# A first stage written as a table of steps, in a kernel of linear attention and a gated unit

## The chip, the core and the metric

One of the eight cores of a Trainium2 chip runs the kernel. The metric is the device time of one execution in microseconds (us), given as the median of several runs. PE is the matrix engine (TensorE), DVE the vector engine, ACT the scalar engine, POOL is GpSimd, and SP is the engine whose queue issues all DMA transfers of this kernel.

## The reference, cut to what matters

```python
xn = _layernorm(x, axis=-1)
qkv = (xn @ wqkv).reshape(B, S, 3, H, Dh)       # S 2048, D 1024, H 32, Dh 32
pq, pk = q @ w_phi, k @ w_phi                   # per head
phi = concat(softmax(p), softmax(-p))           # for q and k
num, den = phi_q (phi_k^T v), phi_q sum(phi_k)
s = (num / den).reshape(B, S, D) @ wo
g = silu((sigmoid(xn @ w_gate) * (xn @ w_up)) @ w_down)   # F 3584
return x + s * g
```

All of it is fp32. The tokens are taken in two chunks of 1024.

## The kernel before, in words

**Products.** Every large product is cut into 2 x 2 blocks, and seven block products, named B11, B21, T2, T3, T4, T1 and B22, take the place of eight; T1 to T4 and B22 have sums of blocks as operands. An fp32 operand is split in two: ACT casts it to its upper half (the helper `split`, L176), DVE subtracts that from the operand and so gets the lower half (L177). `mm3` (L181 to L183) then makes upper x upper, upper x lower and lower x upper. A block product of the first stage has four tiles of 128 tokens with four slices of depth 128 each, so 4 x 4 x 3 = 48 PE products of 128x512. Its results go to one PSUM bank for each tile (`banks[0]` to `banks[3]`) and are evacuated by `proj_out`, by ACT for B11 and B21 (L474, L477), by DVE for the others (L471).

**The first stage.** The first seven of the list `ops` are the block products of V for the first chunk; K's and Q's follow. Beside them the kernel makes ready what they need:

- It loads x in eight tiles of 128 x 1024 (`xk`). Each is normalized: `norm_steps` has DVE take the statistics (L211, L212), then a chain of small steps (L214 to L223) and a scaling of the tile, on ACT (L227) or DVE (L229). PE transposes it in two halves with four transposes each (L249). The halves of tiles 0 to 3 are split from PSUM as operands of B11 and B21 and copied to SBUF (L252). From tiles 4 to 7 and these copies, sums are made for T3 and T2 (`x_tiles`, on POOL), T4 and T1 (`x_late`, on POOL).
- It loads V's weights in four blocks of 1 MB (`v_load`) and makes four sums of them (`v_sums`, L302): three on DVE and T2's on POOL. Each sum is stored to `wf_d` (L303).
- It folds `w_phi` into the weights of K and Q. `fold(which, k)` loads four pieces of 256 KB (`fold_load`, L340), multiplies each by a block-diagonal `bd` on PE (four fp32 products of 128x128, L354, which the profile shows as 8 rows: a fold group), copies the four results to SBUF on ACT (L356, L358), makes two sums on DVE and two on POOL (L79) and stores seven blocks to `wf_d` (L345). There are four folds for K and four for Q.

**What sets the order.** The code puts x's first tile and its first product in front, with 44 transposes of an identity before them (`keep_going`, L844), and the rest into a queue `side`; `step()` runs one entry of it behind each tile of a block product. The helper `Pieces` cuts POOL's sums in pieces of 256 columns (L79). Weights are split ahead by `prep`, in a ring of eight slots. A scheduler then orders the instructions of each engine by its own estimates, but only where data, buffers or an explicit "issue after" leave it a choice. Each engine runs its own list in order; SP too, so that a transfer waits for all that stands before it in SP's list.

Of the kernel before, what the change touches and what calls it, by code (L numbers as in the profile page):

```python
# [17 lines left out]
P = 128  # L18
S, D, H, DH, F = 2048, 1024, 32, 32, 3584
KT = D // P  # L20
# [71 lines left out]
B11, T2, T3, B21, T1, T4, B22 = range(7)  # L92


@with_exitstack
def hedgehog_glu_kernel(
# [92 lines left out]
    side, last_sp = deque(), []  # L189
# [14 lines left out]
    def norm_steps(tiles, xs, scale=None):  # L204
# [20 lines left out]
        for i, xt in enumerate(xs):  # L225
            if scale is None:
                nc.scalar.activation(xt, xt, AF.Identity, bias=b[:, i:i + 1], scale=r[:, i:i + 1])  # L227
            else:
                scale(xt, xt, r[:, i:i + 1], b[:, i:i + 1], op0=ALU.mult, op1=ALU.add)  # L229

    def norm(tiles, xs, scale=None):
        for _ in norm_steps(tiles, xs, scale):
            pass

    def operand(c, i, u, b):

        if c == 0:
            o, cs = run(XO[i], 4), slice(u * P, (u + 1) * P)
            split((o[:, :, 0, cs], o[:, :, 1, cs]), b.rearrange("p (k t) -> p k t", t=P))
        else:  # L240
            nc.sync.dma_start(xo_d[i, :, u], b)

    def transpose(t, xt, dst):

        th, u = t // 4, t % 4
        for q in range(2):
            tp = tps.next()
            for k in range(4):
                nc.tensor.transpose(tp[:, k * P:(k + 1) * P], xt[:, (4 * q + k) * P:(4 * q + k + 1) * P], ident)  # L249
            if th == 0:  # L250
                operand(0, (B11, B21)[q], u, tp)
            nc.scalar.copy(dst[q], tp)  # L252
# [28 lines left out]
    fblock = {K: Ring(((4, 5), (6, 7))), Q: Ring(((50, 51), (52, 53)))}  # L281
# [9 lines left out]

    def v_load(i):
        r, f, kh = ((39, 0, 0), (41, 0, 1), (45, 1, 0), (36, 1, 1))[i]
        nc.sync.dma_start(row4(r), v_block(f, kh))

    def v_sums(*which):
        vec, pl = nc.vector.tensor_tensor, pool.tensor_tensor
        for t, f, o, a, b, op in ((T1, vec, 3, 2, 3, ALU.add), (T3, vec, 2, 0, 2, ALU.subtract),
                                  (T2, pl, 0, 3, 0, ALU.subtract), (B22, vec, 1, 1, 0, ALU.subtract)):
            if t in which:  # L300
                for h in range(2):
                    f(whole(VA[o] + h), whole(VA[a] + h), whole(VA[b] + h), op=op)  # L302
                nc.sync.dma_start(wf_d[V, t], row4(v_first[t]))  # L303
# [29 lines left out]

    fold_raw = {}

    def fold_load(which, k):
        for n in range(4):
            r = fraw.next()
            fold_raw.setdefault((which, k), []).append(r)
            last_sp[:] = [nc.sync.dma_start(r, wqkT[which, n // 2, k + 4 * (n % 2)].rearrange("p g n -> p (g n)")).ins]  # L340

    def fold(which, k):

        def keep(i, b):
            nc.sync.dma_start(wf_d[which, i, :, k], b)  # L345

        if (which, k) not in fold_raw:
            fold_load(which, k)
        a11, a12, a21, a22 = bs = halves(*fblock[which].next())
        for n, (b, r) in enumerate(zip(bs, fold_raw[which, k])):  # L350
            ps = tps.next()
            for g in range(4):
                gs = slice(g * P, (g + 1) * P)
                nc.tensor.matmul(ps[:, gs], r[:, gs], bd[:, 4 * (n // 2) + g], start=True, stop=True)  # L354
            if which == Q:
                nc.scalar.copy(b.rearrange("p (a g d) -> p g a d", a=2, d=DH), ps.rearrange("p (g a d) -> p g a d", a=2, d=DH))  # L356
            else:
                nc.scalar.copy(b, ps)  # L358
        for i, b in ((B11, a11), (B21, a12), (T4, a22)):
            keep(i, b)  # L360
        if k < 3:
            fold_load(which, k + 1)
        vector.add(a22, a21, a22)
        pool.sub(a21, a11, a21)
        vector.sub(a11, a22, a11)
        pool.sub(a12, a12, a11)
        with tc.issue_after(last_sp[0]):
            for i, b in ((T2, a11), (T1, a22), (T3, a21), (B22, a12)):
                keep(i, b)
# [461 lines left out]

    XS = (24, 25, 26, 27, 52, 53, 24, 25)
    first = [halves(i) for i in (50, 51, 54, 38)]
    b12s, b22s = Ring(halves(10)), halves(8, 9)
    xts = [x_load(0, XS[0])]
    v_load(0)
    xts += [x_load(t, XS[t]) for t in range(1, 4)]
    v_load(1)
    xts += [x_load(t, XS[t]) for t in range(4, 6)]

    def keep_going(n):

        for _ in range(n):
            nc.tensor.transpose(banks[3][:, :P], ident, ident)  # L844

    def x_norm(*tiles, scale=None):
        norm(tiles, [xts[t] for t in tiles], scale)

    def x_tiles(*tiles):
        for t in tiles:  # L850
            if t < 4:
                transpose(t, xts[t], first[t])
            else:
                u = t - 4
                (b11, _), (b12, b22) = first[u], (b12s.next(), b22s[u])
                transpose(t, xts[t], (b12, b22))
                pool.sub(b12, b22, b12)
                operand(0, T3, u, b12)
                pool.add(b11, b12, b11)
                operand(0, T2, u, b11)  # L860
            if t < 2:
                xts.append(x_load(t + 6, XS[t + 6]))
            if t == 1:
                v_load(2)
                v_load(3)

    def x_late():
        for u, (b11, b21) in enumerate(first):
            pool.sub(b21, b21, b11)
        block("x6", XO[T4], 4, F32R)  # L870
        for u, (b11, b21) in enumerate(first):
            operand(0, T4, u, b21)
        for u, (b11, b21) in enumerate(first):
            pool.sub(b11, b22s[u], b11)

    def x_rest():
        for i, name, src in ((B22, "x1", b22s), (T1, "x2", [b[0] for b in first])):
            block(name, XO[i], 4, F32R)
            for u in range(4):
                operand(0, i, u, src[u])  # L880
        fraw.items = halves(43, 54)

    with tc.high_priority():
        keep_going(44)
        x_norm(0, scale=nc.vector.tensor_scalar)
        x_tiles(0)
        x_norm(1)
    while prep():
        pass
    one = whole(44)[:, :P]  # L890
    nc.gpsimd.memset(one, 1.0)
    nc.scalar.copy(ones, one)
    phraw = whole(47)[:, :KT * DH].rearrange("p (g f) -> p g f", f=DH)
    nc.sync.dma_start(phraw, w_phi.rearrange("(g p) f -> p g f", p=P))
    nc.gpsimd.memset(bd, 0.0)
    for j in range(4):
        nc.gpsimd.tensor_copy(bd[j * DH:(j + 1) * DH, :, j * DH:(j + 1) * DH], phraw[j * DH:(j + 1) * DH])

    def todo(f, *a, **kw):
        side.append(lambda: f(*a, **kw))  # L900
# [387 lines left out]
```

## Time and profile before

| | |
|---|---|
| median of 3 runs | 2368.73 us (2367.17 to 2371.69) |
| the profiled execution's own time | 2370.45 us |
| its span, first to last instruction | 2368.7 us |
| PE busy | 2346.8 us (99%) |
| DVE, ACT, POOL busy | 1656.8, 992.8, 1189.1 us (70%, 42%, 50%) |
| mean granted clock of PE | 0.997 |
| moved by DMA | 626.24 MB, mean 264 GB/s |

In rows of groups, "out<-in" are the names of tiles, then come shapes, the count, busy time and mean time of one, and the idle time of the engine just before them with what ended it. In rows of stretches each engine has its busy time and, in parentheses, its instructions; then come the granted clock, the share of the 16 DMA engines and GB/s. A busy PE is not PE at its peak, since its products are pipelined: 390 ns are shown for a product, while the next one starts after about 227.

### The profile page before, as it was taken

What the parts mean: (1) busy time and instruction counts of PE and PEld (TensorE: products, weight loads), DVE (VectorE), ACT (ScalarE), POOL (GpSimd) and SP (SyncE); (2) the same over time, 40 slices, a digit from 0 to 9 for tenths busy, and PEclk for the clock granted to TensorE, in tenths of its full rate; (3) what the DMA queues carried; (4) which work ended last, traced back from release to release, by engine and by line L of the source; (5) the groups of instructions that cost most, each with busy time, mean ns of one, the idle gap of its engine ahead of it and who ended that gap; (6) DMA issues with size and microseconds to landing.
All of it is one profiled execution on the core that took longest, in us unless ns stands there. A gap on an engine that the chain in (4) does not pass through costs nothing. (4 is left out here: it accounts for less than half of the span.)

```text
span 2368.7 us, 32568 instructions
## 1 busy us (share of the span) xinstructions
PE 2346.8 (99%) x10772; PEld 1953.9 (82%) x10772; DVE 1656.8 (70%) x2360; ACT 992.8 (42%) x1478; POOL 1189.1 (50%) x1362
## 2 busy tenths in 40 slices
PE   8999999999999999999999999999999999999999
PEld 7788888878888788888888888888888888888887
DVE  7644788677777676466867878776666676667886
ACT  6432344444554454233434344443434333355442
POOL 4510166768776633304363544555444455633767
PEclk9999999999999999999999999999999999999999
DMA  8875566888887889858888877879777877878665
GB/s 299 271 260 175 163 236 220 277 294 300 306 307 275 299 288 364 311 178 275 271 282 274 293 268 259 284 253 356 249 241 260 269 237 244 288 255 291 227 210 168
DMA packets 266427, 626.24 MB, mean 264 GB/s; under 512 B 37905, under 2 KB 66577, under 8 KB 261649
## 3 DMA queue, kind: packets, MB, share of 16 engines
q1 hardware_dynamic: 266256, 624.15, 77.4%
q8 instruction: 85, 1.39, 0.2%
q14 instruction: 86, 0.70, 0.1%
HBM read 374.47 MB, written 249.56 MB: 263 GB/s over the span
## 5 line engine op out<-in xcount | busy, mean ns | idle before, releaser
L182 PE MATMUL bank<-x,w 128*128 128x512 f32 x2352 | 916.2, 390 | 0.0
L181 PE MATMUL bank<-x,w 128*128 128x512 f32 x2352 | 904.9, 390 | 4.5 <-DVE fb L1052 3.3
L183 PE MATMUL bank<-x,w 128*128 128x512 f32 x2352 | 905.8, 389 | 0.0
L79 POOL TENSOR_TENSOR fc<-fc 128x256 f32<-128x256 f32 x494 | 426.7, 894 | 443.1 <-DMA fc<-e_d 105.9
L176 ACT CAST w<-fa 128x512 fp32r<-128x512 f32 (+1 forms) x444 | 308.2, 698 | 561.7 <-PE bank L182 353.2
L177 DVE TENSOR_TENSOR w<-fa,w 128x512 fp32r<-128x512 f32 (+1 forms) x444 | 404.5, 913 | 197.2 <-ACT w L176 191.2
L181 PEld LDWEIGHTS bank<-x,w 128*128 128x128 f32 x2352 | 441.9, 188 | 98.0 <-DVE fb L1052 4.2
L183 PEld LDWEIGHTS bank<-x,w 128*128 128x128 f32 x2352 | 442.1, 188 | 91.6
L182 PEld LDWEIGHTS bank<-x,w 128*128 128x128 f32 x2352 | 442.2, 188 | 90.4
L181 PE MATMUL bank<-w,x 128*128 128x512 f32 x704 | 276.0, 392 | 2.4 <-ACT w L176 1.6
L183 PE MATMUL bank<-w,x 128*128 128x512 f32 x704 | 275.9, 392 | 0.9 <-DVE x L177 0.9
L182 PE MATMUL bank<-w,x 128*128 128x512 f32 x704 | 275.6, 391 | 1.0 <-DVE w L177 1.0
L79 POOL TENSOR_TENSOR fb<-fa 128x256 f32<-128x256 f32 x112 | 100.1, 914 | 244.3 <-DMA fa<-w_gu 143.7
L79 POOL TENSOR_TENSOR fb<-fb,fc 128x256 f32<-128x256 f32 x132 | 122.5, 949 | 115.9 <-DVE fc L1059 115.7
L181 PEld LDWEIGHTS bank<-w,x 128*128 128x128 f32 x704 | 132.7, 189 | 30.4 <-ACT w L176 2.1
L183 PEld LDWEIGHTS bank<-w,x 128*128 128x128 f32 x704 | 132.8, 189 | 28.9 <-DVE x L177 1.8
L182 PEld LDWEIGHTS bank<-w,x 128*128 128x128 f32 x704 | 132.7, 189 | 27.9 <-DVE w L177 1.5
L79 POOL TENSOR_TENSOR fc<-fc,sa 128x256 f32<-128x256 f32 x128 | 97.0, 789 | 98.6 <-issue 89.2
L176 ACT CAST p<-fc 128x512 fp32r<-128x512 f32 x100 | 75.6, 758 | 135.4 <-DVE fc L537 68.4
L177 DVE TENSOR_TENSOR p<-fc,p 128x512 fp32r<-128x512 f32 x100 | 102.0, 1024 | 32.0 <-ACT p L176 31.8
L177 DVE TENSOR_TENSOR x<-fa,x 128x512 fp32r<-128x512 f32 x112 | 92.0, 822 | 41.8 <-ACT x L176 41.8
L176 ACT CAST w<-fb 128x512 fp32r<-128x512 f32 (+1 forms) x114 | 71.2, 626 | 116.7 <-PE bank L182 91.4
(210 smaller groups left out, 2917.3 us busy)
## 6 DMA issues: line engine op xcount, KB each, us to landing
ws_d<-w SPq DMA_DIRECT2D x112, 512.0 KB, 4.3
w<-ws_d SPq DMA_DIRECT2D x112, 512.0 KB, 5.3
fa<-w_gu SPq DMA_DIRECT2D x84, 512.0 KB, 4.8
fa<-h_d SPq DMA_DIRECT2D x84, 512.0 KB, 4.9
fa<-wf_d SPq DMA_DIRECT2D x32, 1024.0 KB, 6.6
h_d<-fc SPq DMA_DIRECT2D x120, 256.0 KB, 4.7
fa<-w_down SPq DMA_DIRECT2D x80, 256.0 KB, 5.0
h_d<-fb SPq DMA_DIRECT2D x76, 256.0 KB, 4.7
```

What stands on the lines that cost most here:

```text
L79: last = self.engine.tensor_tensor(o[:, s], a[:, s], b[:, s], op=op)
L176: nc.scalar.copy(o[0], src)
L177: return nc.vector.tensor_sub(o[1], src, o[0].bitcast(F32))
L181: nc.tensor.matmul(o, a[0], b[0], start=first, stop=False, **kw)
L182: nc.tensor.matmul(o, a[0], b[1], start=False, stop=False, **kw)
L183: nc.tensor.matmul(o, a[1], b[0], start=False, stop=last, **kw)
```

## The change: a table in place of the code's order

A string `FIRST` now lists some 390 steps of the first stage in one order. A loop gives each to `now(what)`, within `turn()`: every instruction that a step makes must be issued behind the last instruction that earlier steps put on the same engine. So each engine keeps the table's order, SP included; instructions from outside the table may still be put between.

The table covers B11, B21, T2, T3 and T4 of V (products in half depth: "a" is upper x upper, "b" the other two), all of x, the folds 0 to 2 of K with their sums and stores (`f`, `fc`, `k`, `kp`, `ks`), the sums of V's weights and their stores (`v`, `vst`) and the splits of T1's weights and operands (`wcast T1`, `wsub T1`, `scast t1`, `ssub t1`). The loop over `ops` skips the first five. K's fold 3 and the four of Q stay in `side`. Further: x's second tile is loaded first and the first in two halves, V's first two blocks in halves; `w_phi` comes in a layout in which one transfer of 128x256 suffices; two of the four copies to `bd` go to ACT; tile 0, 1, 4 and 5 are scaled on DVE, the others on ACT; K's folds have four sets of buffers (two before); V's sum for T1 is made on POOL and T2's on DVE; of the 16 sums of x, DVE makes 14 and POOL 2.

```diff
+FIRST = """
+x1, bn 1 0, x0a, bn 1 1, x0b, bn 0 0, wphi, x3, diag 1, ag 1, add 1, bn 0 1, sqrt 1, diag 0, ag 0, r01, add 0, c 1
...
+    @contextmanager
+    def turn():
+        traced = nc.cur_bb.bb.instructions
+        mark = traced[-1]
+        with ExitStack() as behind:
+            for i in list(turns_last.values()):
+                behind.enter_context(tc.issue_after(i))
+            yield
+        start = next(k for k in reversed(range(len(traced))) if traced[k] is mark) + 1
+        for i in traced[start:]:
+            turns_last[i.engine] = i
...
-    fblock = {K: Ring(((4, 5), (6, 7))), Q: Ring(((50, 51), (52, 53)))}
+    fblock = {K: Ring(((4, 5), (6, 7), (52, 53), (50, 51))), Q: Ring(((52, 53), (50, 51)))}
...
+        elif kind == "v":
+            i, h, p = map(int, a[:3])
...
+            if a[3] == "P":
+                nc.gpsimd.tensor_tensor(columns(o, p), columns(l, p), columns(m, p), op=op)
+            elif p == 3:
+                nc.vector.tensor_tensor(o, l, m, op=op)
...
+        elif kind == "vst":
+            i = (T2, B22, T3, T1)[int(a[0])]
+            nc.sync.dma_start(wf_d[V, i], row4(v_first[i]))
...
+    for what in FIRST.replace("\n", " ").strip().split(", "):
+        with turn():
+            now(what)
+    flow.update(item=12, made=24, used=20)
+    fraw.items = halves(43, 54)
     while prep():
         pass
...
+    for w, k in [(K, 3)] + [(Q, k) for k in range(4)]:
+        side.append(lambda w=w, k=k: fold(w, k))
...
         if kind == "proj":
+            if n < 5:
+                continue
...
-        "w_phi": f(A_w_phi).reshape(D, DH),
+        "w_phi": f(np.asarray(A_w_phi).reshape(KT, P, DH).transpose(1, 0, 2)).reshape(P, KT * DH),
```

**Where instructions move.** In the names below `bank_98` to `bank_105` are the eight PSUM banks, `x_0_92` holds raw tiles of x, `x_0_90` and `x_0_91` are the operands of B11 and B21, `w_93` the split weights, `fa_95`, `fb_96`, `fc_97`, `p_94`, `x_0_87` and `x_0_88` buffers of the first stage. First PE at the start, before:

```order
L844 MATMUL bank_101<-ident 128x128 x44
L249 MATMUL bank_102<-ident,x_0_92 128x128 x4
L249 MATMUL bank_103<-ident,x_0_92 128x128 x4
L987 MATMUL bank_98<-w_93,x_0_90 128x512 x12
L181 MATMUL bank_98<-w_93,x_0_91 128x512
L182 MATMUL bank_98<-w_93,x_0_91 128x512
L183 MATMUL bank_98<-w_93,x_0_91 128x512
```

And PE at the start, now:

```order
L1038 MATMUL bank_101<-ident 128x128 x43
L329 MATMUL bank_105<-fb_96 128x128 x3
L1038 MATMUL bank_101<-ident 128x128
L329 MATMUL bank_105<-fb_96 128x128
L329 MATMUL bank_102<-fb_96 128x128 x4
L977 MATMUL bank_103<-ident,x_0_92 128x128 x4
L977 MATMUL bank_104<-ident,x_0_92 128x128 x4
L995 MATMUL bank_98<-w_93,x_0_90 128x512 x2
L329 MATMUL bank_105<-fb_96,x_0_88 128x128 x4
L977 MATMUL bank_102<-ident,x_0_92 128x128 x4
L995 MATMUL bank_98<-w_93,x_0_90 128x512 x4
```

Two fold groups of K stand before the first tile's transposes, and the first tile's products are cut in pieces with folds and transposes between; before, the first fold came behind product 96.

Second POOL, from the fills of `bd` on, before:

```order
L897 COPY fb_96<-fc_97 32x8x32 x4
L79 TENSOR_TENSOR fa_95<-p_94,fa_95 128x256 x8
L79 TENSOR_TENSOR x_0_88<-x_0_88 128x256 x2
L79 TENSOR_TENSOR fc_97<-x_0_88,fc_97 128x256
L79 TENSOR_TENSOR x_0_88<-x_0_88 128x256 x2
L79 TENSOR_TENSOR fc_97<-x_0_88,fc_97 128x256
L79 TENSOR_TENSOR fc_97<-fc_97 128x256
```

POOL at the same place, now:

```order
L942 COPY fb_96<-fc_97 32x8x32 x2
L1014 TENSOR_TENSOR p_94<-fb_96,p_94 128x256 x8
L79 TENSOR_TENSOR x_0_87<-x_0_87 128x256 x2
L1028 TENSOR_TENSOR fc_97<-fc_97 128x256 x2
L79 TENSOR_TENSOR x_0_87<-x_0_87 128x256 x2
L1028 TENSOR_TENSOR fc_97<-x_0_88,fc_97 128x256
```

The sums of x (`x_0_88`, `fc_97`) have left POOL but for two; counted up to Q's first fold POOL has 22 pieces of 128x256 where it had 56. DVE, behind the scaling of tile 4, now:

```order
L970 TENSOR_SCALAR fc_97<-fc_97,norm_108 128x1024
L1016 TENSOR_TENSOR fb_96<-fa_95,fb_96 128x1024
L970 TENSOR_SCALAR fc_97<-fc_97,norm_108 128x1024
L1030 TENSOR_TENSOR x_0_88<-x_0_88 128x512
L1030 TENSOR_TENSOR fc_97<-x_0_88,fc_97 128x512
L1030 TENSOR_TENSOR fc_97<-fc_97 128x512
```

There the sums of x stand, each in one piece of 512 columns (L1030).

Third SP at the start, before:

```order
L201 DMA x_0_92<-xk 128x1024
L294 DMA fa_95<-wv 128x4x512
L201 DMA x_0_92<-xk 128x1024 x3
L294 DMA fa_95<-wv 128x4x512
L201 DMA fc_97<-xk 128x1024 x2
L894 DMA fc_97<-w_phi 128x8x32
L294 DMA fb_96<-wv 128x4x512
L294 DMA p_94<-wv 128x4x512
```

SP at the start, now:

```order
L259 DMA x_0_92<-xk 128x1024
L928 DMA x_0_92<-xk 128x512 x2
L924 DMA fc_97<-w_phi 128x256
L259 DMA x_0_92<-xk 128x1024
L323 DMA fb_96<-wqkT 128x512 x2
L938 DMA fa_95<-wv 128x2x512
L323 DMA x_0_88<-wqkT 128x512
L938 DMA fa_95<-wv 128x2x512
```

The weights of K's first fold and the small `w_phi` now stand in front of V's second half block; V's first half block stands behind 2.2 MB of other transfers, where the whole block was second. From the 653rd PE instruction on (of 10646) PE's order is the same in both programs; this is behind product 415 and K's, and all of Q's, last fold.

More of the change, by code (lines that the diff above doesn't have):

```diff
@@ L225, in norm_steps @@
         for i, xt in enumerate(xs):
[L226 to L233, printed above, removed]
-    def operand(c, i, u, b):
[L237 to L252, printed above, removed]
+            nc.scalar.activation(xt, xt, AF.Identity, bias=b[:, i:i + 1], scale=r[:, i:i + 1])
+    def operand(c, i, u, b):
+        nc.sync.dma_start(xo_d[i, :, u], b)
     def x_sums(u, first, second):
@@ L867, in x_late @@
[L867 to L881, printed above, removed]
@@ L891, in hedgehog_glu_kernel @@
[L891 to L900, printed above, removed]
-    todo(x_tiles, 1)
-    todo(lambda: (x_norm(2, 3), x_tiles(2, 3)))
```

335 lines of the change are left out of this document (235 added, 100 removed).

## The prediction

> **What bounds it now.** I read first the busy time by stretches, then the groups of the first stretch, then the moments at which the first operands arrive.
>
> ```profile
> span 2368.7 us, 32568 instructions
> core 0: us, PE busy (x) PEld busy (x) DVE busy (x) ACT busy (x) POOL busy (x), PEclk, DMA share, GB/s
> 8.38:26.00 17.62, 13.38 (x50) 9.67 (x49) 16.65 (x39) 10.19 (x17) 2.66 (x4) 0.72 1.07 389
> 26.00:43.50 17.50, 16.96 (x86) 13.69 (x85) 15.49 (x33) 13.04 (x22) 7.42 (x8) 0.99 0.73 288
> 43.50:81.00 37.50, 32.22 (x200) 27.09 (x199) 23.51 (x23) 19.78 (x35) 35.88 (x40) 1.00 0.73 227
> 81.00:111.00 30.00, 29.43 (x165) 25.04 (x163) 18.86 (x26) 14.92 (x24) 8.72 (x9) 1.00 0.82 284
> 111.00:160.00 49.00, 48.57 (x249) 41.46 (x250) 19.55 (x25) 16.05 (x24) 11.45 (x16) 1.00 0.94 324
> ```
>
> The second number is PE's busy time, the last columns the granted clock, the DMA share and GB/s. After 81 us PE is idle 1.0 us of 79. Before it, three things show: DVE fills the first two stretches (32.1 of 35.1 us), the clock is at 0.72 in the first, and POOL fills the third (35.88 of 37.50 us) while PE stands idle for 5.3 us. To size the loss I need the pace of undisturbed work: big products, groups of four transposes, groups of four fold products.
>
> ```profile
> 94.85 0.39 PE L181 MATMUL bank<-w,x 128*128 128x512 f32 x1
> ...
> 102.34 0.39 PE L181 MATMUL bank<-w,x 128*128 128x512 f32 x1
> 82.84 1.06 PE L354 MATMUL bank<-fb,x 128*128 128x128 f32 x8
> 83.73 1.06 PE L354 MATMUL bank<-fb,fc 128*128 128x128 f32 x8
> 84.55 0.48 PE L181 MATMUL bank<-w,x 128*128 128x512 f32 x1
> 41.85 1.91 PE L249 MATMUL bank<-ident,fc 128*128 128x128 f32 x16
> 43.51 0.48 PE L181 MATMUL bank<-w,x 128*128 128x512 f32 x1
> 160.08 0.59 ACT L477 COPY fc<-bank 128x512 f32<-128x512 f32 x1 [2.17 <-PE bank L183]
> ```
>
> The first two rows are 33 products apart: 0.227 us each. Two fold groups take 84.55 - 82.84 = 1.71 us: 0.86 each. Four transpose groups take 1.66 us: 0.415 each. The last row is the end of product 420, the third tile of K's B21: seven products of V make 7 x 4 x 12 = 336, K's B11 and three tiles of B21 another 84. I take this as the yardstick, because by the order of instructions the new program has done the same PE work there and runs the same PE order from there on. The work up to it is 420 x 0.227 + 16 x 0.415 + 32 x 0.86 = 95.3 + 6.6 + 27.5 = 129.4 us. Between 8.38 and 160.05 lie 151.7 us, so the start loses 22.3 us. More than that cannot be won.
>
> ```profile
> L249 PE MATMUL bank<-ident,x 128*128 128x128 f32 x24 | 4.7, 373 | 0.9 <-ACT x L227 0.9
> L987 PE MATMUL bank<-w,x 128*128 128x512 f32 x12 | 3.5, 421 | 0.7 <-DVE w L177 0.5 <-ACT x L176 0.2
> L182 PE MATMUL bank<-w,x 128*128 128x512 f32 x4 | 2.7, 669 | 1.0 <-DVE w L177 1.0
> L183 PE MATMUL bank<-w,x 128*128 128x512 f32 x4 | 2.5, 628 | 0.0
> L181 PE MATMUL bank<-w,x 128*128 128x512 f32 x4 | 2.4, 596 | 1.6 <-ACT w L176 1.6
> ```
>
> That is all of PE's work from 8.38 to 26 us besides two last warm-up transposes: 24 transposes and 24 products, 6 x 0.415 + 24 x 0.227 = 7.9 us of work in 17.6. So 9.7 us of the loss lie here, the other 12.6 behind 26 us, most of them in POOL's stretch.
>
> **The change, part by part. First: the start.** Both programs wait for DMA. In the old one x's first tile and V's first block (1.57 MB) are the first two transfers.
>
> ```profile
> 4.20 1.28 DVE L211 BATCH_NORM_STATS2 bn<-x 128x6 f32<-128x512 f32 x2 [4.20 <-DMA x<-xk]
> 7.11 2.00 ACT L176 CAST w<-fa 128x1024 fp32r<-128x1024 f32 x2 [0.96 <-DMA fa<-wv]
> 9.66 0.74 PE L987 MATMUL bank<-w,x 128*128 128x512 f32 x2 [0.24 <-ACT x L176]
> ```
>
> In the new order 2.75 MB stand up to and with V0a, the half that the first weight split needs. At 389 GB/s behind the 1.57 MB at 7.1 us it lands at 7.1 + 1.18 / 0.389 = 10.1 us. The split's cast (1.0 us, half of the row at 7.11) and a fold copy and the x cast behind it on ACT (0.6 us each) put the first big product at about 12.4 us, 2.7 later than now. PE gets two fold groups and two transpose groups before it (2 x 0.86 + 2 x 0.415 = 2.6 us), so the delay is covered. Behind it DVE sets the pace.
>
> ```profile
> L177 DVE TENSOR_TENSOR w<-fa,w 128x1024 fp32r<-128x1024 f32 x9 | 11.4, 1277 | 1.8 <-ACT w L176 1.6
> L229 DVE TENSOR_SCALAR x<-x,lnw 128x1024 f32<-128x1024 f32 x3 | 2.3, 812 | 0.1
> L220 DVE TENSOR_TENSOR lnw<-lnw 128x1 f32<-128x1 f32 x2 | 0.3, 160 | 0.0
> L177 DVE TENSOR_TENSOR x<-bank,x 128x512 fp32r<-128x512 f32 x8 | 5.2, 674 | 0.0
> ```
>
> Up to the 24th product the table gives it 8 half-tile statistics (0.64 each, by the row at 4.20), 23 small steps of the norms (0.16), 2 scalings, 2 weight splits and 4 x splits: 5.1 + 3.7 + 1.6 + 2.6 + 2.7 = 15.7 us. At 91.5%, DVE's share of the first two stretches, that ends at 4.2 + 15.7 / 0.915 = 21.4 us. By then PE has 24 products, four fold groups and four transpose groups behind it: 10.6 us of work, where the old kernel had 7.9 at 26.0. Lead: 4.6 + 2.7 = 7.3 us, which is part of the sum below and not added to it.
>
> **Second: sums leave POOL.** By the order, 34 quarter-sums of 128x256 leave POOL in this stage, and 17 sums of 128x512 come to DVE.
>
> ```profile
> L79 POOL TENSOR_TENSOR x<-x 128x256 f32<-128x256 f32 x24 | 24.2, 1030 | 14.8 <-ACT x L252 10.6 <-DVE x L79 3.3 <-DMA wf_d<-x 0.9
> L79 POOL TENSOR_TENSOR fc<-x,fc 128x256 f32<-128x256 f32 x12 | 10.4, 885 | 0.0
> 4.20:111.00 106.80, 96.18 (x525) 79.67 (x523) 78.11 (x129) 59.40 (x98) 54.68 (x60) 0.95 0.82 286
> L79 DVE TENSOR_TENSOR x<-x 128x512 f32<-128x512 f32 x8 | 8.1, 1016 | 7.8 <-POOL x L79 5.6 <-DMA wf_d<-x 2.0
> L177 DVE TENSOR_TENSOR x<-fc,x 128x512 fp32r<-128x512 f32 x9 | 8.3, 941 | 4.7 <-ACT x L176 4.2
> L177 DVE TENSOR_TENSOR x<-x,x 128x512 fp32r<-128x512 f32 x8 | 7.4, 958 | 6.0 <-ACT x L176 6.0
> 110.97 0.68 DVE L471 TENSOR_TENSOR fc<-fc,bank 128x512 f32<-128x512 f32 x1
> ```
>
> POOL loses 34 x 0.96 = 33 us of its 54.7 and is no bound any more; what comes next is DVE. It has 78.1 us of work up to T4's last evacuation at 111 us. The 17 sums cost 0.69 us each if they run like the split that reads PSUM (674 ns above) and 1.02 if like the sums beside a busy POOL: 11.7 to 17.3 us. I take the low end, since POOL has little left. By the same reason the old operations that read SBUF twice (1016, 941 and 958 ns) may fall to about 0.69: 8 x 0.33 + 9 x 0.25 + 8 x 0.27 = 7.0 us less. That leaves 78.1 + 11.7 - 7.0 = 82.8 us. Of these, three of T4's evacuations and one of T1's weight splits (3 x 0.68 + 1.23 = 3.3 us) stand behind T4's last product: 79.5 us. At the same 91.5% they take 86.9 us, and T4 ends at 4.2 + 86.9 = 91.1 us. PE alone would need 240 products, 16 transpose and 16 fold groups (K's fourth block is drawn forward): 54.5 + 6.6 + 13.8 = 74.9 us, from 8.38 to 83.3.
>
> The Trainium skill, SBUF — State Buffer, Who interferes with whom, says that a DVE operation with two SBUF inputs and a GpSimd operation that reads SBUF block each other, and one with a PSUM input does not; the rows agree (941 to 1016 ns against 674). By the rule the whole 7.0 us are saved, which is what I count; without it T4 would end at 98.7.
>
> **Third: the tail.** Behind T4's end 180 products and Q's 16 fold groups remain: 40.9 + 13.8 = 54.7 us, plus 1.5 us, twice the idle share of the two late stretches. The DMA queue adds to it. From 111 to 160 us it is 94% busy, and PE waits for fold weights:
>
> ```profile
> PE bank L354 <- DMA x<-wqkT: 1.8, 2, 1.4
> PE bank L354 <- DMA fc<-wqkT: 0.8, 1, 0.8
> ```
>
> The same bytes must pass in less time, so I allow two such waits of 0.9 us: 1.8 us. The stores of V's and K's sums and T1's weight split, now steps, cost nothing of their own: other engines issue or run them beside products, and their price if that cover goes is the third rival. The yardstick falls at 91.1 + 54.7 + 1.5 + 1.8 = 149.1 us instead of 160.05: 11.0 us won. The profiled execution took 2370.45 us, of which its span is 2368.7; it would take 2359.5. It lies 1.7 us above the median of the runs, 2368.73, so that I predict 2357.7 us.
>
> **Bounds.** With DVE at the 94.5% of its first stretch (16.65 of 17.62), T4 ends at 88.3; without the 1.8 us for DMA the gain is 15.6. With the moved sums at 1.02 and no relief, T4 ends at 4.2 + (79.5 + 5.6 + 7.0) / 0.915 = 104.9 and 2.8 us are lost. The low end needs a POOL that is as busy as before, so I keep the range nearer to the other.
>
> **Rivals.** (1) The clock falls again.
>
> ```profile
> 9.14:12.56 3.42, 2.71 (x12) 1.54 (x11) 3.42 (x6) 1.13 (x3) 0.00 (x0) 1.00 1.03 396
> 12.56:15.97 3.41, 1.54 (x5) 0.70 (x5) 3.41 (x9) 2.75 (x4) 0.00 (x0) 1.00 1.07 373
> 22.80:26.21 3.41, 3.41 (x17) 3.33 (x18) 3.41 (x5) 3.41 (x6) 0.00 (x0) 0.50 1.24 390
> ```
>
> After a stretch of 3.41 us with PE busy for 1.54 the clock halves, and it comes back only behind one that is full. In the new order I get 2.2 to 2.8 busy in such a stretch of the first 20 us: between the rows. One fall costs half of 6.8 to 10.2 us, 3.4 to 5.1; the time would be about 2362. Chance 0.09. The Trainium skill, TensorE: Matmul & The Clock Gate, Part 1, lets the clock fall after a window of about 3.4 us that is idle; the second row was only half idle, so the trace is stricter. By the page no window here would fall.
>
> (2) The fixed order itself. Each engine waits at its own place, and a late operand now holds all behind it, DVE's queue above all. If DVE is busy for no more than 80%, T4 ends at 4.2 + 79.5 / 0.80 = 103.6, and with the same tail nothing much is left: 161.6, 2370 us. For it: DVE is at 63% in POOL's stretch. Against: there POOL is what it waits for. Chance 0.14, with a few hundredths of it for the case that the gain is given back behind product 420 because K's or Q's operands come no earlier.
>
> (3) Slower: the SP queue. Stores of sums stand in front of loads of fold weights there, and a store waits for its sum. Should each of the 28 fold groups behind K's first block find its weights late by the 0.87 us of the three waits quoted above, 24 us are lost; with 11.0 won the time is 2382. It is slower than now from 13 such waits on. For it: DMA is the busiest queue of the tail. Against: the new order issues each fold block's loads about a block ahead. Chance 0.08.
>
> **How the numbers follow.** Forecast 0.69, (1) 0.09, (2) 0.14, (3) 0.08. A measurement of this kernel can tell about 0.2%, 4.7 us, from no change. The forecast, most of (1) and a little of neither side give faster 0.77; (2) and the rest of (1) give same 0.15; slower 0.08. The range holds the forecast with its upper bound (2353) and a margin for the relief being larger, and reaches down through (1) into the start of (2): 2351.5 to 2366.5.
>
> **What would show it.** Product 420 (the third copy of K's B21) near 149 us instead of 160; T4's last evacuation near 92 instead of 111; the 24th product before 22 us; POOL below 25 us up to T4's end; sums and splits from SBUF near 0.69 us; DVE busy around 90% up to T4. Wrong if DVE has holes behind DMA or ACT, if the clock is at 0.5 for more than one such window, or if PE waits for fold weights for more than 3 us.

## The result, and the profile after

| | before | after |
|---|---|---|
| median of 6 runs each, on one chip | 2369.93 us | 2358.23 us (2357.15 to 2359.73) |
| ratio, 95% interval | | 0.995 [0.994, 0.9961] |
| the profiled execution, its span | 2370.45, 2368.7 us | 2357.55, 2355.8 us |
| mean granted clock of PE | 0.997 | 1.000 |

The kernel is 11.7 us faster; the forecast was 2357.7 us, 11.0 less than the median it started from. Here are the stretches of the first stage after the change, with the columns as before and T4's end at 91 us as one more cut:

```profile
8.38:26.00 17.62, 16.41 (x105) 13.72 (x104) 14.77 (x34) 13.82 (x24) 0.00 (x0) 1.00 1.05 397
26.00:43.50 17.50, 17.50 (x106) 14.95 (x105) 15.83 (x30) 13.05 (x25) 7.03 (x10) 1.00 0.63 231
43.50:81.00 37.50, 35.78 (x193) 29.92 (x191) 32.17 (x42) 20.30 (x34) 17.70 (x8) 1.00 0.80 293
81.00:91.00 10.00, 10.00 (x51) 8.39 (x50) 9.24 (x16) 5.19 (x9) 0.00 (x0) 1.00 0.28 100
91.00:111.00 20.00, 18.37 (x105) 15.74 (x104) 11.71 (x17) 6.31 (x9) 2.87 (x4) 1.00 1.00 361
111.00:149.00 38.00, 38.00 (x210) 32.95 (x209) 13.09 (x16) 14.18 (x23) 9.34 (x12) 1.00 0.97 329
```

PE is busy for 16.41 us of the first stretch (13.38 before, at a clock of 0.72). POOL is down to 17.70 us in the third, and PE is idle there for 1.7 us instead of 5.3. From PE's timeline after the change come the rows at product 240, the end of T4's products, and at product 420:

```profile
86.67 4.15 PE L995 MATMUL bank<-w,x 128*128 128x512 f32 x17
90.66 0.38 PE L329 MATMUL bank<-fb,fc 128*128 128x128 f32 x2
...
148.01 0.39 PE L226 MATMUL bank<-w,x 128*128 128x512 f32 x1
148.24 0.39 PE L224 MATMUL bank<-w,x 128*128 128x512 f32 x1
```

Product 240 is the last of the 17 in the first row, and the next work starts at 90.66 us. Product 420 is the one at 148.01, with its successor at 148.24; before, the successor starts at 159.84 (the prediction's 160.05 lies by the start of its evacuation). So 11.6 us of the gain lie ahead of product 420. The spans differ by 12.9; the rest is mostly a single window of half clock at 784 us that this execution of before has and this one of after has not (last section).

To see where in the stage the time was won, I count PE's work up to a product at the pace given in the prediction (0.227 us for a product, 0.415 for a transpose group, 0.86 for a fold group) and take it from the product's end less 8.38 us. At product 240 after the change: 240 x 0.227 + 16 x 0.415 + 15.8 x 0.86 = 74.7 us of work, and 90.66 - 8.38 - 74.7 = 7.6 us lost. In the same way for each kernel of this study, in us lost since 8.38:

| up to product | 24 | 48 | 96 | 144 | 240 | 336 | 420 |
|---|---|---|---|---|---|---|---|
| before | 6.7 | 11.0 | 11.2 | 16.3 | 20.5 | 21.9 | 22.0 |
| after | 3.7 | 4.2 | 4.9 | 6.1 | 7.6 | 10.1 | 10.4 |
| e13, after once more | 3.1 | 3.7 | 4.5 | 5.6 | 6.7 | 10.8 | 11.0 |
| e1, no order | 3.7 | 3.8 | 7.2 | 15.5 | | | 18.2 |
| e10, order on PE | 4.1 | 9.2 | 17.8 | 21.6 | 21.9 | 22.4 | 22.4 |
| e9, order on DVE | 4.5 | 5.1 | 6.1 | 13.4 | 14.0 | 14.7 | 15.0 |
| e11, order on PE and DVE | 5.9 | 6.2 | 9.0 | 11.2 | 11.4 | 12.0 | 12.2 |
| e3, sums on POOL | | | 7.4 | 10.8 | 11.6 | | 14.9 |
| e4, folds late | 7.1 | | | | | | 14.0 |
| e7, half the statistics | 3.2 | 3.8 | 4.3 | 5.4 | 6.3 | 8.8 | 9.0 |
| e6, T1's weights free | 3.6 | 4.2 | 5.2 | 6.4 | 7.9 | 8.4 | 8.6 |

After against before: 3.0 us are won up to product 24, 3.8 more up to 48, 3.4 more up to 144 and 2.7 more up to 240; 1.3 are given back in the tail. The row of e13, a second profile of the changed kernel, shows how far two executions of one kernel lie apart: up to 0.9 us.

On DVE, up to 91 us, these are the groups that answer to the sums and splits shown of before, then two groups of POOL, then that stretch as a whole:

```profile
L919 DVE TENSOR_TENSOR x<-fc,x 128x512 fp32r<-128x512 f32 x8 | 5.9, 749 | 0.8 <-ACT x L916 0.8
L919 DVE TENSOR_TENSOR x<-x,x 128x512 fp32r<-128x512 f32 x8 | 5.5, 683 | 4.2 <-ACT x L916 4.2
L79 DVE TENSOR_TENSOR x<-x 128x512 f32<-128x512 f32 x6 | 4.1, 678 | 0.0
L1030 DVE TENSOR_TENSOR fc<-x,fc 128x512 f32<-128x512 f32 x5 | 3.4, 684 | 0.0
```

```profile
L1028 POOL TENSOR_TENSOR fc<-fc 128x256 f32<-128x256 f32 x2 | 6.9, 3494 | 13.5 <-DVE fc L1030 13.5
L79 POOL TENSOR_TENSOR fc<-fc 128x256 f32<-128x256 f32 x2 | 6.1, 3056 | 10.5 <-DMA wf_d<-fc 10.5
```

```profile
4.20:91.00 86.80, 83.88 (x471) 71.16 (x470) 75.63 (x131) 53.13 (x90) 25.50 (x20) 1.00 0.77 281
```

The splits went from 941 and 958 ns to 749 and 683, the old sums from 1016 to 678, and the sums that came to DVE take 684. Of POOL's few pieces, four take 3.1 to 3.5 us each, where the mean before was about 0.96.

### The profile page after: what moved, and what is told of

Same layout as the page of the kernel before. It is cut to its first block, busy times and chain, and to the rows that moved or that the text cites. A ratio compares the mean times of both kernels' runs of the same rounds, so it can differ in the third digit from the quotient of the medians.

```text
span 2355.8 us, 32533 instructions
## 1 busy us (share of the span) xinstructions
PE 2339.2 (99%) x10772; PEld 1950.1 (83%) x10772; DVE 1663.0 (71%) x2371; ACT 989.3 (42%) x1478; POOL 1162.5 (49%) x1326
## 5 line engine op out<-in xcount | busy, mean ns | idle before, releaser
L220 DVE TENSOR_TENSOR w<-fa,w 128x512 fp32r<-128x512 f32 (+1 forms) x436 | 395.7, 910 | 200.0 <-ACT w L219 185.1
L219 ACT CAST w<-fa 128x512 fp32r<-128x512 f32 (+1 forms) x436 | 300.0, 691 | 556.9 <-PE bank L225 343.3
L226 PEld LDWEIGHTS bank<-x,w 128*128 128x128 f32 x2352 | 441.5, 188 | 91.5
L224 PE MATMUL bank<-w,x 128*128 128x512 f32 x628 | 244.9, 390 | 0.4 <-DVE fc L506 0.4
L225 PE MATMUL bank<-w,x 128*128 128x512 f32 x628 | 244.7, 390 | 0.0
L226 PE MATMUL bank<-w,x 128*128 128x512 f32 x628 | 244.3, 389 | 0.0
L224 PEld LDWEIGHTS bank<-w,x 128*128 128x128 f32 x628 | 118.0, 188 | 24.7 <-DVE fc L506 0.6
L226 PEld LDWEIGHTS bank<-w,x 128*128 128x128 f32 x628 | 117.9, 188 | 24.4
L225 PEld LDWEIGHTS bank<-w,x 128*128 128x128 f32 x628 | 118.0, 188 | 23.5
L219 ACT CAST w<-fb 128x512 fp32r<-128x512 f32 x112 | 69.0, 617 | 115.8 <-PE bank L225 91.3
```

Of the source, the lines that this page charges most:

```text
L219: nc.scalar.copy(o[0], src)
L220: return nc.vector.tensor_sub(o[1], src, o[0].bitcast(F32))
L224: nc.tensor.matmul(o, a[0], b[0], start=first, stop=False, **kw)
L225: nc.tensor.matmul(o, a[0], b[1], start=False, stop=False, **kw)
L226: nc.tensor.matmul(o, a[1], b[0], start=False, stop=last, **kw)
```

## The experiments

Each was timed in five rounds beside the kernel before on the same chip (before: 2369.31, 2369.25 and 2370.02 us in the three groups, e1 to e4, e5 to e9, e10 to e13, against 2369.93 above: a difference between medians of two groups is uncertain by such 0.8 us). My theory was the prediction's: the start is filled, sums leave POOL, and DVE's work at some 90% share sets T4's end. The rivals were that the fixed order does nothing or harms, that the DMA queue decides, and later that PE itself bounds the stage.

**e1: the steps without a binding order.**

```diff
         with ExitStack() as behind:
-            for i in list(turns_last.values()):
-                behind.enter_context(tc.issue_after(i))
             yield
```

> The table's steps are issued in the table's order in the program, but no step is bound to stand behind the last one on its engine; the scheduler orders each engine as it likes. Theory A (the gain comes from what the table holds: which engine makes which sum, what is loaded first, folds as early work for PE; the binding itself is worth little): 2356 to 2361 us. Theory B (the gain comes from the binding, since the scheduler's estimates are what put holes into the start): 2364 us or more.

Measured: 2367.46 us (2364.23 to 2369.5), ratio 0.999 [0.9981, 0.9999]. Theory B holds: the same instructions on the same engines, left to the scheduler, give back 9.2 of the 11.7 us. The table shows where: the start is as good as with the order, and 11.7 us are lost between products 48 and 144 where the bound kernel loses 1.9. PE's longest wait, from the list of waits, and the two stretches:

```profile
PE bank L975 <- DVE fc L968: 5.4, 1, 5.4
```

```profile
26.00:43.50 17.50, 15.35 (x81) 12.14 (x80) 14.02 (x24) 11.78 (x19) 9.61 (x11) 1.00 0.88 326
43.50:81.00 37.50, 32.12 (x180) 28.23 (x179) 34.06 (x53) 21.83 (x37) 12.80 (x8) 0.91 0.72 263
```

PE stands for 5.4 us, from 46.03 to 51.41 us, before the transposes of tiles of x that DVE has not scaled yet, and in that wait the clock falls (0.91). DVE is not short of time: it has 14.02 us of work in the 17.50 us ahead. It does other things first. This is what DVE's timeline of e1 has there:

```profile
43.79 1.76 DVE L1014 TENSOR_TENSOR fa<-fa 128x1024 f32<-128x1024 f32 x1
...
46.08 1.21 DVE L917 TENSOR_TENSOR w<-fa,w 128x1024 fp32r<-128x1024 f32 x1
47.22 1.22 DVE L917 TENSOR_TENSOR w<-fb,w 128x1024 fp32r<-128x1024 f32 x1
...
50.54 1.54 DVE L968 TENSOR_SCALAR fc<-fc,norm 128x1024 f32<-128x1024 f32 x2
```

And the first of these scalings after the change:

```profile
35.83 0.81 DVE L970 TENSOR_SCALAR fc<-fc,norm 128x1024 f32<-128x1024 f32 x1
```

Sums of V's weights and splits of weights for later products, 1.2 to 1.8 us each, pass the short steps of the norm of tiles 4 to 7, and the scaling comes 14.7 us later than in the table's order.

**e9, e10, e11: the order on some engines only.** `turn()` records the last instruction of the named engines alone, so that only they keep the table's order; the line is that of e9, with PE in place of DVE in e10 and both in e11:

```diff
         for i in traced[start:]:
-            turns_last[i.engine] = i
+            if i.engine in (mybir.EngineType.DVE,):
+                turns_last[i.engine] = i
```

> The changed kernel with the order of the table binding on VectorE alone: turn() records only VectorE's last instruction, so that PE, ACT, GpSimd and SP are ordered by the scheduler. With no engine bound the time was 2367.5 us, with all bound 2358.2. Theory A: VectorE is the queue whose order matters, since PE's waits of the middle are waits for VectorE's results (the scaling of an x tile, 5.4 us at one place without binding); bound alone it gives back most of the 9 us: 2358 to 2361 us. Theory B: the order of PE or ACT matters as much (products run ahead of the transposes and folds that later work needs): 2363 us or more. Between the two, both matter.

> The changed kernel with the order of the table binding on PE alone: turn() records only PE's last instruction, the other engines are ordered by the scheduler. No engine bound gave 2367.5 us, VectorE alone 2362.2, all 2358.2; bound on VectorE alone, PE ran 96 products by 44.8 us (all bound: 49.5) with 8 groups of transposes done instead of 16, and lost 7.3 us over the next 48. Theory A: the other half of what binding brings is PE's, which has to make transposes ahead of products that it could already run; bound alone it gives what VectorE's doesn't, about 4 of the 9 us: 2362 to 2365 us. Theory B: PE's order is worth something only when the results that it waits for come in the table's order too: PE then stands in front of transposes whose input VectorE makes late, and the time is 2366 us or more.

> The changed kernel with the order of the table binding on PE and VectorE, free on ACT, GpSimd and SP. Theory A: these two are the engines that wait and are waited for in the first stage, so nothing is lost: 2357 to 2360 us. Theory B: ACT's order matters as well, since its splits of x and its scalings feed both (PE waits for x from ACT and for VectorE's scaling): 2361 us or more.

Measured: e9 2362.2 us (2360.17 to 2365.34), ratio 0.9973 [0.9962, 0.9984]; e10 2370.09 (2366.9 to 2371.28), ratio 1.0 [0.9991, 1.0009]; e11 2361.07 (2358.18 to 2361.99), ratio 0.9956 [0.9942, 0.997]. For e9 this is just above theory A's range and below theory B's, so both orders matter: DVE's alone brings 5.3 of the 9.2 us. For e10 theory B holds: an order on PE alone brings nothing (its median is 2.6 us above e1's, which the intervals hardly tell apart), and the whole gain over before is gone. PE's waits of e10 from 20 to 85 us and its third stretch show how:

```profile
PE bank L978 <- DVE fc L971: 5.7, 1, 5.7
PE bank L978 <- ACT x L973: 3.2, 1, 3.2
PE bank L330 <- DMA fb<-wqkT: 3.0, 2, 1.6
```

```profile
43.50:81.00 37.50, 30.43 (x174) 26.49 (x175) 31.31 (x51) 25.55 (x44) 12.96 (x8) 0.91 0.78 257
```

PE now waits in the table's order for tiles (scaled on DVE, L971, and on ACT, L973) that the other engines make in another one. In e9 PE's order is free and its waits are short, but it does products first: 8 of 16 transpose groups by product 96, then one wait of 2.6 us for fold weights, a fall of the clock, and 7.3 us lost up to product 144. With both bound (e11) 5.0 us are lost there, less than the 8.3 of e9 from product 48 on but more than the 1.9 of after; behind product 144 most of that is won back, and 1.8 us are left at product 420 against after. PE's longest waits of e11 from 8 to 75 us:

```profile
PE bank L996 <- ACT x L917: 2.0, 1, 2.0
PE bank L978 <- DVE fc L971: 1.6, 1, 1.6
PE bank L330 <- ACT x L981: 1.1, 1, 1.1
```

The first is at the start. On ACT, which is free in e11, the cast of the second half of the weights (13.29 us) comes before the cast of x that PE waits for (14.24); in the table's order that cast of x is first, at 12.98. The wait of 2.0 us costs a window of half clock as well, and product 24 is 2.2 us later. The other two end at 40.55 and 55.27 us. The median of e11 lies at the edge of theory B's range (2361 or more), but two of its five runs, 2358.18 and 2358.29 us, are as fast as after: what ACT's order is worth stays open.

**e2: the kernel before, with 14 of the 16 sums of x and V's T2 sum moved from POOL to DVE, T1's sum to POOL.**

```diff
-                pool.sub(b12, b22, b12)
+                vector.sub(b12, b22, b12)
-                pool.add(b11, b12, b11)
+                vector.add(b11, b12, b11)
...
-            pool.sub(b21, b21, b11)
+            (pool if u == 2 else vector).sub(b21, b21, b11)
```

> The kernel before, with only the sums moved as the change moves them: 14 of the 16 sums of x and V's sum for T2 on DVE, V's sum for T1 on POOL. Theory A (POOL's full stretch from 43.5 to 81 us is what PE waits for there): POOL below 70% in that stretch, 4 to 6 us of the 5.3 us of PE's idle time and of its slow pace there go, and the time is 2363 to 2366 us. Theory B (POOL is busy but something else, DMA or the folds' buffers, ends the waits): within 2 us of the kernel before, or slower, since DVE has 10 to 17 us more to do.

Measured: 2374.19 us (2369.65 to 2377.15), ratio 1.002 [1.0011, 1.0029]: slower than before, which is theory B's time, though what theory A says of POOL's stretch came true. The stretches of e2, and its longest wait of PE:

```profile
43.50:81.00 37.50, 35.39 (x212) 29.90 (x210) 29.90 (x41) 20.25 (x34) 9.48 (x10) 1.00 0.66 214
81.00:111.00 30.00, 25.27 (x133) 20.92 (x132) 10.39 (x15) 8.35 (x14) 9.17 (x11) 0.94 0.97 294
```

```profile
PE bank L354 <- DMA fb<-wqkT: 5.5, 3, 2.4
```

POOL was indeed what held the stretch from 43.5 to 81 us: freed, PE is busy for 35.39 us there instead of 32.22. But the next stretch gives it back: the DMA engines are 97% busy, PE waits for fold weights and the clock falls. In us lost, by the count above, e2 is 2.5 better than before at product 144 and 4.9 worse at 420. So this move alone is worth nothing. That the fold work and its loads stand in other places in the table is what I take to make the difference there; no run tried that alone.

**e3: the changed kernel, with DVE's sums of x on POOL.**

```diff
-xT3 0 0 D, ... xT3 0 1 D, xT2 0 0 D, ... xT1 0 1 D
+xT3 0 0 P, ... xT3 0 1 P, xT2 0 0 P, ... xT1 0 1 P
```

> The changed kernel with all 16 sums of x on POOL, in pieces of 256 columns at the same places of the table. Theory A: 28 more pieces of 0.74 to 1.0 us, 21 to 28 us more on POOL, in a stretch where operands of T3 and T2 wait for them: T4's end comes 5 to 8 us later and the time is 2363 to 2367 us. Theory B (sums were not the bound, the order was): within 2 us of the changed kernel.

Measured: 2363.07 us (2361.68 to 2366.76), ratio 0.9976 [0.9967, 0.9986]: 4.8 us of the 11.7 are gone, within theory A's range, though T4's products end at 94.19 us, 3.5 later and not the 5 to 8 expected. Its third stretch, and the groups of DVE up to 91 us:

```profile
43.50:81.00 37.50, 32.45 (x174) 27.09 (x172) 33.67 (x30) 18.48 (x30) 36.09 (x31) 1.00 0.68 237
```

```profile
L922 DVE TENSOR_TENSOR x<-fc,x 128x512 fp32r<-128x512 f32 x7 | 7.9, 1144 | 0.8 <-ACT x L919 0.8
L79 DVE TENSOR_TENSOR x<-x 128x512 f32<-128x512 f32 x6 | 6.2, 1039 | 0.0
L922 DVE TENSOR_TENSOR x<-bank,x 128x512 fp32r<-128x512 f32 x8 | 5.3, 672 | 1.2 <-ACT fc L983 1.2
```

POOL is the bound again (36.09 of 37.50 us), and beside it DVE's operations that read SBUF twice take 1144 and 1039 ns instead of 749 and 678, while the split that reads PSUM stays at 672. (The eight splits `x<-x,x` take 754 ns on average against 683; the last four of them, behind POOL's last piece at 82 us, take no more than 690 ns again.) DVE's work in that stretch is 33.67 us with 12 instructions fewer than the 32.17 us of after.

**e4: the changed kernel, with the folds of the start (`f 0 1`, `f 0 0`, `f 0 3`) and their copies behind the first tile's products.**

```diff
-V0a, f 0 1 3, ... apply 0 D, f 0 0 0, ... fc 0 1, ... fc 0 0, ... f 0 3 3
+V0a, ... apply 0 D, ... copy 1 0, f 0 1 3, fc 0 1, f 0 0 2, fc 0 0, f 0 3 3
```

> The changed kernel with the three fold groups that stand before and within the first tile's products moved behind the first tile's products. Theory A (they fill a time in which PE has nothing else, and so also keep the clock up): PE stands idle from 8.6 to about 11 us and again before the first product, the granted clock falls to a half for 6.8 to 10.2 us, and 2.6 us of folds are paid for later: 5 to 8 us slower than the changed kernel, 2363 to 2366 us. Theory B (DVE paces the start and PE has room for them later): less than 2 us slower.

Measured: 2362.84 us (2359.64 to 2366.26), ratio 0.9974 [0.9964, 0.9984]: 4.6 us slower than after, just short of theory A's 5 to 8. Two windows of its start:

```profile
11.11:14.53 3.42, 0.89 (x4) 0.30 (x2) 2.16 (x4) 3.17 (x5) 0.00 (x0) 1.00 1.05 392
14.53:17.94 3.41, 2.91 (x10) 2.42 (x11) 2.88 (x5) 1.91 (x3) 0.00 (x0) 0.50 1.04 395
```

Without folds PE is busy for 0.89 us while it waits for V0a, and the clock is at half for the next 3.41 us. The 3.4 us lost by product 24 stay to the end (3.6 at product 420). The prices of e1, e3 and e4 (9.2, 4.8 and 4.6 us) are more than 11.7 together, so they are not shares of the gain.

**e5: the stores of V's and K's sums outside `turn()`; e6: T1's weights left to `prep`, as before; e12: both.** The first three added lines are e5's, the rest is e6's; in the rows of the table here and below, the steps between are left out.

```diff
     for what in FIRST.replace("\n", " ").strip().split(", "):
+        if what.split()[0] in ("vst", "kp", "ks"):
+            now(what)
+            continue
...
-wcast T1 0, ... wcast T1 1, ... wsub T1 1, ... wsub T1 0
-    flow.update(item=12, made=24, used=20)
+    flow.update(item=10, made=20, used=20)
```

> The changed kernel, with the stores of v's and k's sums (the steps vst, kp and ks) still issued at their places in the table, but outside turn(): they are not bound to the steps before and after them on SP's queue. Theory A, mine: these stores have room wherever they stand, since until 91 us the DMA engines are busy 69% of the time and the tail's waits for fold weights are 2.5 us in all; the time stays within 2 us of the changed kernel's 2358.2 us (2356 to 2360). Theory B, the stores' places matter, as the third rival of the prediction has it: unbound they go ahead of fold weights in SP's queue, PE waits for fold weights longer than 2.5 us, and the time is 2362 us or more.

> The changed kernel without the two casts and two subtractions of T1's weights as steps of the table: the prep of the next products makes them after the first stage, as it does for B22's. Theory A: PE has T4's products to run while they are made and the tail bears them; the time stays within 2 us of 2358.2 us. Theory B: T1's first product waits for them, or for the prep's other work behind them on ACT and DVE, by a cast of 0.6 us and a subtraction of 0.7 us twice, about 2.6 us, and with B22's weights moved back by as much, up to 5 us: 2361 to 2363 us, and the loss shows between product 240 and product 336.

> The changed kernel with the stores of v's and k's sums outside turn() and T1's weights left to the prep, the two edits that alone gave 2358.2 and 2355.6 us. Theory A: the gain of the second is real, since product 420 ended 1.8 us earlier in its trace and PE had no wait for fold weights left in the tail, and the first adds nothing: 2355 to 2357 us, below the changed kernel of this call by 1.5 us or more. Theory B: the 2.6 us were the scatter of the runs: 2357.5 us or more.

> The changed kernel once more, for comparison on the same chip with the other three: 2357 to 2360 us by either theory.

Measured: e5 2358.17 us (2356.87 to 2361.13), ratio 0.9956 [0.9944, 0.9969]; e6 2355.62 (2354.68 to 2359.58), ratio 0.9948 [0.9934, 0.9962]; e12 2356.62 (2355.41 to 2357.81), ratio 0.9943 [0.993, 0.9955]; the changed kernel again, e13, 2357.56 (2357.32 to 2359.22), ratio 0.9948 [0.9935, 0.996]. In e5 the stores did move: the first two go out at 14.2 and 16.9 us, ahead of fold weights that they followed in after. Their place in the order is worth nothing, as theory A had it. T1's weights as steps bring nothing either; they may cost something: without them product 420 ends 1.8 us earlier in the trace and PE has no wait left from 90 to 150 us, against the 1.3 us for fold weights and 0.4 for a bank that after has there. Whether the two edits together make a faster kernel stays open: 2356.62 against 2357.56 is less than I asked for, and the intervals lie over each other.

**e7: the changed kernel, with 4 us less work for DVE.**

```diff
-bn 3 1, ... bn 2 1, ... bn 4 1, ... bn 5 1, ... bn 7 1, ... bn 6 1
...
-                nc.vector.bn_aggr(mv[:, :, i], st[:, i])
+                nc.vector.bn_aggr(mv[:, :, i], st[:, i] if t < 2 else st[:, i, :1])
```

> The changed kernel with less work for VectorE: for the tiles 2 to 7 of the first stage the statistic of the second half row (step bn t 1) is left out, and mean and variance are those of the first half. Six statistics of about 0.67 us leave VectorE, 4 us of its 75.6 us up to T4's end; PE's work, its order and the DMAs stay. Theory A, as the prediction had it: VectorE's work over a share near 90% sets the end of T4, so T4 ends 3 to 4.5 us earlier and the time is 2353.5 to 2355.5 us. Theory B, what the trace after seems to say: from product 24 to product 240 PE has 64.1 us of work in 68.05 us, so PE bounds the stage and only the rest can shrink: the gain is under 2 us, 2356.2 us or more.

This kernel leaves out half of the statistics of tiles 2 to 7, so its output is not the reference's; it serves for its time alone. Measured: 2357.51 us (2356.14 to 2357.94), ratio 0.9951 [0.9938, 0.9963], 0.7 us below after and level with e13. The statistics are 8 instead of 12 in that group, and T4's products end at 89.34 us, 1.3 us sooner than in after's profile and 0.4 sooner than in e13's (89.73), as PE's timeline of e7 shows:

```profile
L951 DVE BATCH_NORM_STATS2 norm<-x 128x6 f32<-128x512 f32 x8 | 5.3, 686 | 5.8 <-DMA x<-xk 5.7
```

```profile
85.35 4.15 PE L997 MATMUL bank<-w,x 128*128 128x512 f32 x17
89.34 0.38 PE L331 MATMUL bank<-fb,fc 128*128 128x128 f32 x2
```

Theory B holds: DVE is not what sets T4's end. DVE's own timeline agrees: in after it stands idle for 4.16 us before 79.95 us, waiting for a cast of ACT, and in e7 for 3.51 us at the same place.

## Why the prediction was right, and where it was right by luck

**The start.** The order of events was as forecast, later by about a microsecond: the first big product started at 13.62 us (forecast 12.4), because V0a landed at 11.55 (forecast 10.1). In e13, the same kernel, its cast starts at 11.03, so about half a microsecond is scatter; x came 0.35 us later too (4.55 instead of 4.20). The rest I have not settled. The 24th product ended at 22.60 with the forecast work done (10.5 us), so the lead over what before had lost by 26 us is 9.7 - 3.7 = 6.0 us instead of 7.3. What the step left unpriced is the clock: it lists a fall only as a rival, but the start's gain hangs on there being none. Before, PE was busy for 8.6 of 10.24 us at half clock, which cost it some 4.3 us; in e4, without the folds in the gap, the clock falls there.

**POOL and the relief.** These sizes were right. From 4.20 to 91 us POOL was busy for 25.50 us, near the 25 given, though four pieces took three times their usual time. The sums on DVE took 0.68 us as at the low end taken. The relief of the old operations is 8 x 0.338 + 9 x 0.192 + 8 x 0.275 = 6.6 us against 7.0, and e3, which puts POOL's load back, brings the long times back for operations with two inputs in SBUF and not for those from PSUM. That is the rule of the Trainium skill, SBUF — State Buffer, Who interferes with whom, and here an experiment, no longer only rows side by side, agrees with it.

**DVE as the next bound: the step that failed.** The prediction has T4 end at 4.2 + 79.5 / 0.915 = 91.1 us, and T4's products ended at 90.66. But DVE had 75.63 us of work up to 91 us, not 79.5, and was busy for 87% of the time, not 91.5%: two errors that cancel. That is luck. Part of the first is plain: 5.3 us of its work that the table has beside T4 lay behind 91 us, where I had put 3.3. And e7, with 4 us less of that work, ended T4 only 0.4 to 1.3 us sooner. What the runs show in its place is PE: between products 24 and 240 it has 64.2 us of work in 68.06 us, so that T4's end is the 74.7 us of PE's work plus the 3.7 us lost at the start and 3.9 us lost behind it. Of these the list of waits shows 1.9 (1.2 for fold weights, 0.5 for a weight split of DVE, 0.2 for a scaling on ACT); the rest is spread over places where PE shows no wait. The prediction had this number, 83.3 us for PE alone, as a lower limit; it should have been the base of the sum, with the losses added to it. The forecast was met because the losses of 3.7 and 3.9 us that it had not added to PE's sum are nearly as long as the 7.8 us by which DVE's sum lay above it.

**T4's last evacuation** "near 92" was wrong, without a consequence. These are its four evacuations, from DVE's timeline after the change:

```profile
91.57 0.68 DVE L506 TENSOR_TENSOR fc<-fc,bank 128x512 f32<-128x512 f32 x1
95.04 0.68 DVE L506 TENSOR_TENSOR fc<-fc,bank 128x512 f32<-128x512 f32 x1
98.23 0.69 DVE L506 TENSOR_TENSOR fc<-fc,bank 128x512 f32<-128x512 f32 x1 [1.37 <-DMA qkv_d<-fc]
105.13 0.69 DVE L506 TENSOR_TENSOR fc<-fc,bank 128x512 f32<-128x512 f32 x1 [1.86 <-DMA qkv_d<-fc]
```

They stand behind T1's weight splits and wait for the stores of earlier results; PE waited 0.4 us for a bank through it.

**The tail.** From T4's end to product 420 it took 57.6 us (forecast 58.0). PE's two waits for fold weights up to 150 us are these:

```profile
PE bank L329 <- DMA fc<-wqkT: 1.3, 1, 1.3
PE bank L329 <- DMA fb<-wqkT: 1.2, 1, 1.2
```

Only the first, which ends at 94.07 us, is in the tail, so 1.3 us stand against the 1.8 allowed; the second ends at 78.06, ahead of T4's end. (The expectation of e5 puts both into the tail.)

**The rivals.** (1) The clock did not fall in after's profile, but it fell once in the tail of e13, the same kernel, and in the first stage of e4, e9, e10, e11 and e1. A fall there lasted one window of 3.41 us, or two in e1 and once in e10: at most 1.7 or 3.4 us, where the prediction gave it 3.4 to 5.1. Nor does the clock come back only behind a full window: in e4 it did behind the one with 2.91 us busy that is shown above. What decides a fall is in the last section. (2) That the fixed order costs time: e1 says the opposite, without it 9.2 of the 11.7 us are gone. Its argument was not empty, though. e10 is this rival: order on one engine, and late operands hold all behind it. The prediction counted the order as a risk only and never as a source of gain; it was right about the total because it took the table's order as given. (3) Stores before loads in the DMA queue: not here, since freeing the stores (e5) changes nothing. In e2 PE waits 6.6 us in all for fold weights (5.5 for `fb`, 1.1 for `x`); that stores held them up there is not shown.

## What to carry to other kernels

An order written out by hand paid in full here only when all engines kept it, those that wait and those that are waited for: on PE alone it brought nothing, on DVE alone 5.3 of 9.2 us, on both 6.4. Moving work off a bounding engine can be worth nothing when the next stretch gives the time back (e2: the bound went, and the time rose by 4.9 us). When a forecast rests on one engine's share of busy time, work out the other candidate's sum as well, with its losses; if the two ends lie within a few us, a run with less work on one of them tells which.

## What the runs showed of the hardware

**The clock goes by windows with a fixed phase, and half a window of idleness is enough.** In all fourteen traces the changes of clock lie whole multiples of 3.41 us behind the first release. The same wait of PE for a result of DVE (L1180 in after), near 770 us, shows it; it takes 2.6 us in before and 2.5 in e3. First before, where most of it falls into one window and the clock is at half in the next, then e3, where an edge cuts it in two and the clock stays:

```profile
780.56:783.97 3.41, 1.22 (x5) 1.05 (x6) 3.41 (x6) 1.15 (x2) 3.41 (x5) 1.00 0.90 357
783.97:787.39 3.42, 3.42 (x9) 2.67 (x8) 2.88 (x5) 1.73 (x2) 3.42 (x4) 0.50 0.88 195
```

```profile
770.09:773.51 3.42, 2.28 (x11) 1.55 (x9) 1.55 (x3) 0.00 (x0) 3.42 (x6) 1.00 0.95 373
773.51:776.92 3.41, 2.09 (x9) 1.74 (x10) 3.41 (x5) 1.14 (x2) 3.41 (x4) 1.00 0.88 345
```

I laid such windows over every trace of this study: of some 9,600 at full clock, 18 were followed by one at half (the end of the program left out). PE was busy for 1.81 us or less in all of these; no window with less than 1.53 us kept the clock, and none with more than 1.81 lost it. Between the two both happened. The clock came back behind windows at half clock with 2.91 us busy or more and stayed at half behind those with 2.7 or less. A window at half clock costs about 1.7 us of work. In e13, the changed kernel again, a wait for a bank (0.4 us) and one for fold weights (1.2) meet in one window:

```profile
90.73:94.14 3.41, 1.80 (x13) 1.33 (x12) 3.41 (x6) 1.31 (x3) 0.00 (x0) 1.00 0.93 297
94.14:97.55 3.41, 3.41 (x10) 2.65 (x10) 2.29 (x4) 1.07 (x2) 0.00 (x0) 0.50 1.06 304
```

The first release lay anywhere from 5.4 to 8.4 us, so the windows fall differently in each execution. That this is the scatter of 2 to 3 us between executions of one kernel is likely, not shown. The Trainium skill, TensorE: Matmul & The Clock Gate, Part 1, speaks of a window that is idle; here a half idle one was enough.

**A few POOL pieces beside a busy DVE take 3.1 to 3.5 us instead of about 1.** The two engines hinder each other: with much work on POOL DVE's operations grow by half (e3), with much on DVE the rare POOL piece grows to three times its length. In e3, where DVE has fewer such operations, the pieces of the same two groups take 1.1 and 1.5 us. PE waited for none of them here.
